# Attention and two MLPs in one launch: the second MLP tile taken from batch 1, plain fp32 P^T V for the early parts, and half-width transposes of the last 64 queries

## The chip, the core and the metric

One core of a Trainium2 chip runs the whole program in one launch. The engines are named as in the profile: PE (TensorE, matmuls and transposes), PEld (its weight loads), DVE (VectorE), ACT (ScalarE), POOL (GpSimd) and SP (SyncE, whose queue issues nearly all transfers). The metric is the device time in microseconds (us).

## The reference

Four batches, eight heads, 576 positions, head size 64; then two MLPs, 512 to 2048 to 512, over all 2304 tokens.

```python
scores = q @ k.T / 8 + minimum(-(cum[i] - cum[j]), 0)   # cum = cumsum(max(s, 0)); causal mask
x = softmax(scores) @ v                                   # -> (2304, 512)
h = x @ w_in;  g = maximum(h, 0) + log1p(exp(-abs(h)));  x = g @ w_out
h = x @ w_in2; P = a0 + a1*h + a2*h*h + a3*h*h*h; Q = 1 + |b0|*|h| + |b1|*h*h
out = (P / (Q + 1e-6)) @ w_out2
```

The MLP weights arrive as 64-bit floats (512 KB for each half of a 128-wide slice of the 2048 hidden features).

## The kernel before

**Numbers on PE.** Most matmuls use the type fp32r. A value that needs more bits is split in two fp32r tiles, a high one (an ACT copy) and a low one (a subtraction on DVE or POOL), and a product is made of three matmuls (the two MLPs) or two (attention, where high and low lie stacked in the 128 rows). A few matmuls take plain fp32 operands ("plain" parts): a matmul of that type appears in the trace as two instructions.

**MLP 1.** A unit is one token tile T and one of 16 feature slices ff: `stage_a` makes h with 12 matmuls, stages 1 to 3 apply the softplus and split it, `stage_b` adds 12 matmuls into the accumulators. The token tiles `T1` have 256, 256 and then four times 448 tokens. The order of the units is T=0 with ff 0 to 7, T=1 with ff 0 to 7, then ff 8 to 15 with T=0 and T=1 in turn, then tiles 2 to 5. Tiles 0 and 1 are the tokens 0 to 255 and 256 to 511 of batch 0. `conv1` turns a 64-bit weight half into a high tile (kept in tag W) and a low tile (written to `l_d` in HBM and fetched again by `stream_l` for later tiles).

**MLP 2** has six tiles of 384 tokens and starts when MLP 1 is nearly done.

**Attention.** A Part is one head and one range of queries. Kind M: queries 0 to 255; L: 0 to 383; B: 256 to 383; H: 384 to 575. `s1` and `s2` make scores and the softmax (DVE minimum and mask, ACT exponential, DVE reciprocal, POOL scaling), `t1` and `t2` transpose the probabilities on PE and `evac_pt` copies them out of PSUM, `pv` multiplies by V. `prep` splits q, k and v in high and low. The parts stand in five segments: M of batch 0 (plain, before any MLP unit); B and H of batch 0; L of batch 1; H of batch 1 with L of batch 2; H of batch 2 with L and H of batch 3. `GROUPS` says over which MLP units a segment is spread: the second over units 0 to 7, the third over units 8 to 31. For kind H, `t2` transposes 128 queries at a time although only the last 64 are new; the copy takes the 64.

**Start.** `load_s0`, `make_cum0` and `load_cum` make the cumulative bias of the first 256 positions of batch 0 and put it as two more rows under q and k of each head, by a transfer from tile to tile. `make_cum` does the same for everything else.

**Order of the work.** `plan` is a list scheduler that simulates all instructions with a table of costs and ties each engine's instructions to the order it found, for those that it starts before a given time (530 us). PSUM has eight banks: four `acc`, two `h`, two `at`. Attention takes `at` and `acc` in turn in the first units (`second_bank`, until unit 10) and `at` alone after.

Of the kernel before, what the change touches and what calls it, by code (L numbers as in the profile page):

```python
# [31 lines left out]
GROUPS = [(0, 8), (8, 24), (32, 16), (48, 16)]  # L32
# [64 lines left out]
class Step:  # L97


    def __init__(self, i, tied):  # L100
# [12 lines left out]
        elif self.engine == "PE":  # L113
            turn = n == 128 and self.ins[0].tile.startswith("ident")
            full = not turn and "32r" not in str(i.ins[0].bass_ap.dtype)
            self.busy = 0.109 if turn else 0.024 + 0.00162 * n if full else 0.012 + 0.000428 * n
# [22 lines left out]
def depend(steps):  # L139
# [4 lines left out]
    for k, s in enumerate(steps):  # L144
# [4 lines left out]
        for x in s.ins + s.outs:  # L149
            if not x.ordered:  # L150
                continue
            write = x in s.outs
            for j, w, y in seen.get(x.tile, ()):
                if (write or w or x.psum and steps[j].engine != s.engine) and x.meets(y):
                    add(j, True)
# [167 lines left out]
def moe_chain_kernel(ctx, tc, qk0, qk, vv, s0, s, w1, w2, ab, out):  # L323
# [62 lines left out]
    class Part:  # L386
        def __init__(self, b, h, kind, rng, first, plain):
            self.b, self.h, self.kind, self.rng = b, h, kind, rng
            self.fresh, self.first, self.plain = rng is not None, first, plain

    def cols(t, rng):
        if rng[0] == "pre":
            return t[:, :, 0:rng[1]]
        return t.rearrange("p a s -> p (a s)")[:, rng[1]:]

# [31 lines left out]
    def load_s0():  # L427
        cum_t["s0"] = sb.tile([2 * H, M + 4], F32, tag="tmp", bufs=1, name="s0_t")
        nc.sync.dma_start(out=cum_t["s0"], in_=s0)

    def make_cum0():
        st, cst = cum_t["s0"][:, 0:M], cum_t["s0"][:, M:M + 4]
        one = t_w("one", [2 * H, M], F32)
        nc.vector.memset(one, 1.0)
        t = t_w("cum0", [2 * H, 2, M], F32)
        nc.vector.tensor_scalar(t[:, 0], st, 0.0, 8.0, op0=ALU.max, op1=ALU.mult)
        nc.vector.tensor_tensor_scan(t[:, 1], one, t[:, 0], 0.0, op0=ALU.mult, op1=ALU.add)
        cum_t["c"] = t_w("cumc", [2 * H, 2, M], F32)
# [3 lines left out]
    def load_s():  # L442
        st = t_w("s_t", [128, S + 6], F32)
        nc.sync.dma_start(out=st, in_=s)
        one = t_w("ones", [128, S], F32)
        nc.gpsimd.memset(one, 1.0)
        cum_t["s"] = (st, one)

    def make_cum():
# [10 lines left out]
        rows = t_q("rows", [128, 2, S], F32R)  # L460
# [5 lines left out]
    def load_pair(i):  # L466
        t = t_w("raw2", [128, 2, 2, M], F32)
        nc.sync.dma_start(out=t[0:64], in_=qk0[i])
        raw2[i] = t

    def load_cum(i):
        for j in range(2):
            h = 2 * i + j
            nc.sync.dma_start(out=raw2[i][64:66, j], in_=cum_t["c"][2 * h:2 * h + 2])

    def load_v0():
        t = t_w("v2", [128, 4, 2, 2, D], F32)
        nc.sync.dma_start(
            out=t.rearrange("p i r c d -> p i (r c d)"),
            in_=vv[0, :, :, 0:2].rearrange("i p r c d -> p i (r c d)"))  # L480
        v2["raw"] = t

    def prep_pair(i):
        for j in range(2):
            op_t[0, 2 * i + j] = (raw2[i][0:66, j], None, v2["raw"][:, i])

    def load_raw(p):
        if p.fresh and p.plain:
# [4 lines left out]
            if p.vkey not in v_t:  # L493
                n = -(-p.rng[1] // 128) if p.rng[0] == "pre" else 5
# [4 lines left out]
        elif p.fresh:  # L499
# [4 lines left out]
            if p.vkey not in v_t:  # L504
                n = -(-p.rng[1] // 128) if p.rng[0] == "pre" else 5
                vr = tmp_tile("R", 2, (128, 5, 2, D))
                nc.sync.dma_start(out=vr[:, 0:n], in_=vv[p.b, p.h // 2, :, 0:n])
                v_t[p.vkey] = [vr, None, n]

    def prep(p):  # L510
        if p.first:
            if p.h % 2 == 0:
                prep_pair(p.h // 2)
        elif p.fresh and not p.plain:
# [3 lines left out]
            if p.rng[0] == "pre":  # L518
                qs = ks = slice(0, p.rng[1])
            else:  # L520
# [56 lines left out]
    def p_tile(p, tag):  # L577
        if p.first:
# [44 lines left out]
    def t1(p):  # L623
        p.pt = (sb.tile([128, 384], F32, tag="pt", bufs=2, name="pt"),) if p.plain else (pt_h[p.idx % 2], pt_l[p.idx % 2])
# [3 lines left out]
        if p.kind in "LM":  # L628
            for i, c0 in enumerate((256, 0, 128)):
                nc.tensor.transpose(bk[:, i * 128:(i + 1) * 128], p.p1[:, c0:c0 + 128], ident)  # L630
            evac_pt(p.pt if p.plain else [t[:, 192:576] for t in p.pt], bk[:, 0:384], nc.scalar)
        else:
            for c in range(4):
                nc.tensor.transpose(bk[:, c * 128:(c + 1) * 128], p.p1[:, c * 128:(c + 1) * 128], ident)
            evac_pt(
                [t[:, 256:1024].rearrange("p (c q) -> p c q", c=4)[:, :, 0:128] for t in p.pt],
                bk.rearrange("p (c q) -> p c q", c=4), nc.scalar)

    def t2(p):
# [3 lines left out]
        if p.kind in "LB":  # L643
            for i in range(3):
                nc.tensor.transpose(bk[:, i * 128:(i + 1) * 128], p.p2[:, i * 128:(i + 1) * 128], ident)
            evac_pt([t[:, 576:960] for t in p.pt], bk[:, 0:384])
        else:

            for i, k0 in reversed(list(enumerate((448, 0, 128, 256, 384)))):
                nc.tensor.transpose(bk[:, i * 64:(i + 2) * 64], p.p2[:, k0:k0 + 128], ident)  # L650
            evac_pt(
                [t[:, 64:1024].rearrange("p (c q) -> p c q", c=5)[:, :, 128:192] for t in p.pt],
                bk[:, 64:384].rearrange("p (c q) -> p c q", c=5))

    def pv(p):
        bk = abank()
        hd = p.h % 2
        ops = []
        for t in p.pt:
            if p.plain:  # L660
                if p.kind == "L":
                    blk = t[:, 64:960].rearrange("p (b q) -> p b q", b=7)
                    ops.append((0, t[:, 320:704], bk[:, 0:384]))
                    ops.append((1, blk[:, 1:6:4, :], bk[:, 128:384].rearrange("p (b q) -> p b q", b=2)))
                    ops.append((2, t[:, 832:960], bk[:, 256:384]))
                elif p.kind == "M":
                    ops.append((0, t[:, 128:384], bk[:, 0:256]))
                    ops.append((1, t[:, 0:128], bk[:, 128:256]))
                elif p.kind == "B":
                    for c in range(3):  # L670
                        ops.append((c, t[:, 576 + c * 128:704 + c * 128], bk[:, 128:256]))
                else:
                    for c in range(4):
                        ops.append((c, t[:, 256 + c * 192:448 + c * 192], bk[:, 64:256]))
                    ops.append((4, t[:, 192:256], bk[:, 192:256]))
# [15 lines left out]
        for i, (c, mv, o) in enumerate(ops):  # L691
            vc = p.vs[:, c] if p.plain else p.vs[:, c, 2 * hd:2 * hd + 2, :]
# [10 lines left out]
        if p.plain:  # L703
# [5 lines left out]

    SPLIT = {  # L710
        "L": [("L", ("pre", 384))],
        "M": [("M", ("pre", 256))],
        "H": [("H", ("suf", 384))],
        "BH": [("B", ("suf", 256)), ("H", None)],
# [3 lines left out]
    def parts_of(lst, first=False, plain=False):  # L718
        return [Part(b, h, k, r, first, plain) for b, heads, kind in lst for h in heads for k, r in SPLIT[kind]]
# [109 lines left out]
    def conv1(ff, half, keep):  # L829
# [5 lines left out]
        if keep:  # L835
            li_t[0, ff, half] = l
            if ff >= NF // 2:
# [46 lines left out]
    def segments(T):  # L884
        t0, m = T1[T]
        o = 0
        while o < m:
            b, s0 = divmod(t0 + o, S)
            n = min(m - o, S - s0)
            yield b, s0, n, o  # L890
            o += n
# [104 lines left out]
    def evacuate(ph, T, acc):  # L996
# [10 lines left out]
        for m, a in enumerate(acc):  # L1007
# [18 lines left out]
            else:  # L1026
                r0 = t0 + m * 128
                nc.sync.dma_start(out=out[r0:r0 + 128, :], in_=yb[:, m % 2])
# [62 lines left out]
    if True:  # L1091
        nc.scalar.preload_act_table_set("natural_log_exp_and_others")
        load_s0()
        load_pair(0)
        load_pair(1)
        load_v0()
        make_cum0()
        load_cum(0)
        load_cum(1)
        for i in (2, 3):  # L1100
            load_pair(i)
# [7 lines left out]
        for i in range(2):  # L1109
            for lst, nm in ((pt_h, "pth"), (pt_l, "ptl")):  # L1110
# [228 lines left out]
```

## Time and profile before

| | |
|---|---|
| median of 3 runs | 1061.16 us (1061.08 to 1062.5) |
| profiled execution | 1063.84 us, span 1062.0 us |
| PE busy | 1022.1 us (96%), 5732 matmuls |
| PEld, DVE, ACT, POOL busy | 923.9, 799.9, 824.1, 462.1 us |
| transfers | 139.43 MB, mean 131 GB/s |
| first unit of tile 0, of tile 2, of MLP 2 on PE | 36.40, 212.28, 663.73 us |

Read the table with care: a PE that counts as busy is not a PE at its peak, because the tail of each matmul, in which the next one already runs, counts too. What a matmul costs is the distance from its start to the next start.

### The profile page before, as it was taken

Reading aid. Unit: us, or ns where it says so; the run is one execution under the profiler, and the core shown is the slowest. Engines: PE = TensorE matmul, PEld = TensorE weight load, DVE = VectorE, ACT = ScalarE, POOL = GpSimd, SP = SyncE. Lnnn points to the kernel's source line nnn. Section 1 sums busy time; section 2 is a strip of 40 time slices with the busy share of each in tenths; the row PEclk is TensorE's granted clock in tenths of the full one; section 3 lists DMA queues with packets and bytes.
Section 4 is the critical chain, followed back from the end, with each engine's and each line's share of the span. In section 5 each row is a group of like instructions: output and inputs, shape, how many; then the busy total and the mean of one; then the engine's idle time right before and its main releaser. Section 6 shows DMA issues by size and latency. Waiting matters only on the chain.

```text
span 1062.0 us, 17769 instructions
## 1 busy us (share of the span) xinstructions
PE 1022.1 (96%) x5732; PEld 923.9 (87%) x5732; DVE 799.9 (75%) x1886; ACT 824.1 (78%) x1748; POOL 462.1 (44%) x509
## 2 busy tenths in 40 slices
PE   5888799999999999999999999999999999999998
PEld 4777699998989888889999888988999999999996
DVE  6898977978886888876666677777676776776765
ACT  5999899987886887875556556787888887888875
POOL 4575365522221122221444575454445454454452
PEclk9899899999999999999999999999999999999999
DMA  6876575755565654415878875110000100000000
GB/s 197 271 240 208 176 239 182 242 168 162 156 179 145 186 172 136 138 56 163 260 232 281 288 248 176 44 31 31 1 31 30 31 31 1 31 31 1 31 1 30
DMA packets 70333, 139.43 MB, mean 131 GB/s; under 512 B 8384, under 2 KB 24144, under 8 KB 70240
## 3 DMA queue, kind: packets, MB, share of 16 engines
q1 hardware_dynamic: 67696, 134.14, 39.3%
q10 hardware_dynamic: 2544, 4.16, 1.6%
q8 instruction: 45, 0.74, 0.3%
q14 instruction: 48, 0.39, 0.1%
HBM read 111.60 MB, written 22.61 MB: 126 GB/s over the span
## 4 chain that ended last, share of the span: by engine, by line
PE 76%; DVE 7%; ACT 6%; DMA 5%; issue 2%; POOL 2%; SPq 0%; POOLq 0%; DVEq 0%; ACTq 0%
PE h L947 7%; PE h L948 7%; PE h L949 7%; PE acc L992 6%; PE acc L990 6%; PE acc L991 6%; PE at L693 5%; PE acc L984 4%; PE acc L985 4%; PE acc L983 4%; PE at L947 4%; PE at L949 4%; PE at L948 3%; DMA raw<-in_w_dram 3%; PE at L569 3%
## 5 line engine op out<-in xcount | busy, mean ns | idle before, releaser
L947 PE MATMUL h<-xs,w1h 128*128 128x448 f32 (+1 forms) x352 | 119.9, 342 | 3.8 <-DVE e L1049 3.8
L949 PE MATMUL h<-xs,w1l 128*128 128x448 f32 (+1 forms) x352 | 118.7, 338 | 1.0 <-POOL w1l L825 1.0
L948 PE MATMUL h<-xs,w1h 128*128 128x448 f32 (+1 forms) x352 | 119.3, 339 | 0.1
L985 PE MATMUL acc<-gh,w1l 128*128 128x448 f32 (+1 forms) x352 | 118.4, 338 | 0.4 <-POOL w1l L825 0.3
L983 PE MATMUL acc<-gh,w1h 128*128 128x448 f32 (+1 forms) x352 | 118.7, 340 | 0.0
L984 PE MATMUL acc<-gl,w1h 128*128 128x448 f32 (+1 forms) x352 | 118.5, 338 | 0.0
L563 POOL TENSOR_SCALAR PA<-PA,stat 128x384 f32<-128x384 f32 (+3 forms) x112 | 71.4, 644 | 102.3 <-DVE stat L562 41.4
L992 PE MATMUL acc<-w2h,gl 128*128 128x512 f32 x288 | 113.5, 394 | 0.0
L990 PE MATMUL acc<-w2h,gh 128*128 128x512 f32 x288 | 113.3, 393 | 0.2 <-ACT gh L1085 0.2
L991 PE MATMUL acc<-w2l,gh 128*128 128x512 f32 x288 | 113.3, 393 | 0.0
L1087 POOL TENSOR_TENSOR gl<-PA,gh 128x384 fp32r<-128x384 f32 x95 | 97.8, 1030 | 6.2 <-ACT gh L1085 5.0
L1058 POOL TENSOR_TENSOR tc<-tc,e 128x384 f32<-128x384 f32 x47 | 51.0, 1085 | 96.4 <-ACT tc L1056 96.4
L563 POOL TENSOR_SCALAR P<-P,stat 128x576 f32<-128x576 f32 x32 | 25.6, 801 | 136.8 <-DVE stat L561 55.6
L947 PEld LDWEIGHTS h<-xs,w1h 128*128 128x128 f32 x352 | 66.6, 190 | 8.5 <-DVE e L1049 5.3
L621 DVE TENSOR_TENSOR ptl<-at,pth 128x320 fp32r<-128x320 f32 (+2 forms) x107 | 60.4, 569 | 15.8 <-ACT pth L620 14.6
L560 ACT ACTIVATE PA<-PA,stat 128x384 f32<-128x384 f32 (+3 forms) x112 | 63.8, 570 | 10.0 <-DVE stat L547 9.5
L949 PEld LDWEIGHTS h<-xs,w1l 128*128 128x128 f32 x352 | 66.4, 188 | 4.2 <-POOL w1l L825 1.3
L984 PEld LDWEIGHTS acc<-gl,w1h 128*128 128x128 f32 x352 | 66.7, 190 | 3.4 <-POOL gl L1087 0.3
L985 PEld LDWEIGHTS acc<-gh,w1l 128*128 128x128 f32 x352 | 66.3, 189 | 3.8 <-POOL w1l L825 0.8
L948 PEld LDWEIGHTS h<-xs,w1h 128*128 128x128 f32 x352 | 66.6, 189 | 3.0 <-DVE xs L917 0.3
L983 PEld LDWEIGHTS acc<-gh,w1h 128*128 128x128 f32 x352 | 66.3, 189 | 2.9
L1085 ACT ACTIVATE gh<-PA 128x384 fp32r<-128x384 f32 x96 | 50.4, 525 | 20.0 <-DVE PA L1073 16.4
(226 smaller groups left out, 3239.6 us busy)
## 6 DMA issues: line engine op xcount, KB each, us to landing
w1l<-l_d SPq DMA_DIRECT2D x148, 256.0 KB
raw<-in_w_dram SPq DMA_DIRECT2D x48, 512.0 KB
raw<-in_qk_dram SPq DMA_DIRECT2D x32, 384.0 KB
l_d<-w1l SPq DMA_DIRECT2D x32, 256.0 KB
raw64x<-in_w_dram SPq DMA_DIRECT2D x16, 512.0 KB
R<-in_vv_dram SPq DMA_DIRECT2D x16, 320.0 KB
raw<-in_qk_dram SPq DMA_DIRECT2D x8, 576.0 KB
out_dram<-yb SPq DMA_DIRECT2D x17, 256.0 KB
```

The costliest lines, as they stand in the source:

```text
L560: nc.scalar.activation(pt[:, 0:n], pt[:, 0:n], AF.Exp, bias=mn, scale=-1.0, accum_out=stat[:, i, 1:2])
L563: nc.gpsimd.tensor_scalar(pt[:, 0:n], pt[:, 0:n], stat[:, i, 2:3], 1.0, op0=ALU.mult, op1=ALU.mult)
L947: nc.tensor.matmul(h, wh[:, cs], xh, start=(k == 0), stop=False)
L948: nc.tensor.matmul(h, wh[:, cs], xl, start=False, stop=False)
L949: nc.tensor.matmul(h, wl[:, cs], xh, start=False, stop=(k == KD - 1))
L983: nc.tensor.matmul(o, wh[:, cs], gh, start=first and not both, stop=False)
L984: nc.tensor.matmul(o, wh[:, cs], gl, start=False, stop=False)
L985: nc.tensor.matmul(o, wl[:, cs], gh, start=False, stop=last and (not both or m % 2 == 1))
L990: nc.tensor.matmul(acc[m], gh[:, cs], wh, start=first, stop=False)
L991: nc.tensor.matmul(acc[m], gh[:, cs], wl, start=False, stop=False)
L992: nc.tensor.matmul(acc[m], gl[:, cs], wh, start=False, stop=last)
L1087: eng.tensor_tensor(gl, g, f(gh), op=ALU.subtract)
```

## The change

Tile 1 of MLP 1 becomes the first 256 tokens of batch 1. The tokens are walked in the order `ORDER`, so tile 2 holds queries 256 to 575 of batch 0 and 256 to 383 of batch 1. Batch 1 gets M parts like those of batch 0 (plain), and its queries 256 to 383 become B parts; its L parts go. The order of units becomes T=0 with ff 0 to 3, T=1 with ff 0 to 3, then ff 4 to 15 with both in turn; M of batch 1 is spread over units 0 to 3, and B and H of batch 0 with B of batch 1 over units 4 to 31. `pv` of M, and of B and H in that segment, works in plain fp32: one copy out of PSUM instead of a split, V used as it is loaded, and the result copied by DVE alone. Two heads of an M pair are added up in one bank (V is loaded with 64 zero columns between the heads), and the bank is split straight into the MLP's input. `t2` of every H part transposes only the rows 64 to 127. At the start the first pair's bias is a matmul of its own (two rows) instead of a transfer; the other pairs' transfers are issued by ACT; the memsets of `ones`, `pth` and `ptl` and `make_cum` come after the first step of the stream. The planner pins the order up to 700 us.

```diff
+ORDER = [(0, 0, 256), (1, 0, 256), (0, 256, 320), (1, 256, 320), (2, 0, S), (3, 0, S)]
+N_S0 = 92
+HF = 4
-GROUPS = [(0, 8), (8, 24), (32, 16), (48, 16)]
+GROUPS = [(0, 4), (4, 28), (32, 16), (48, 16)]
...
+    def fill():
         one = t_w("ones", [128, S], F32)
         nc.gpsimd.memset(one, 1.0)
-        cum_t["s"] = (st, one)
+        cum_t["s"] = (cum_t["s"], one)
+        for i in range(2):
+            for lst, nm in ((pt_h, "pth"), (pt_l, "ptl")):
+                t = t_j(nm, [128, 1024], F32R)
+                nc.gpsimd.memset(f(t[:, 0:192]), 0.0)
+                lst.append(t)
...
     def load_cum(i):
+        eng = nc.scalar if i < 4 else nc.sync
         for j in range(2):
-            h = 2 * i + j
-            nc.sync.dma_start(out=raw2[i][64:66, j], in_=cum_t["c"][2 * h:2 * h + 2])
+            h = 60 + 4 * i + 2 * j
+            eng.dma_start(out=raw2[i][64:66, j], in_=cum_t["c"][h:h + 2])
...
     def scores(o, p, q0, k0, n):
         if p.plain:
-            nc.tensor.matmul(o, p.ht[:, 0, q0:q0 + 128], p.ht[:, 1, k0:k0 + n], start=True, stop=True)
+            nc.tensor.matmul(
+                o, p.ht[:, 0, q0:q0 + 128], p.ht[:, 1, k0:k0 + n], start=True, stop=p.st is None)
+            if p.st is not None:
+                c = cum_t["c"][p.st:p.st + 2]
+                nc.tensor.matmul(o, c[:, 0, q0:q0 + 128], c[:, 1, k0:k0 + n], start=False, stop=True)
             return
...
-            for i, k0 in reversed(list(enumerate((448, 0, 128, 256, 384)))):
-                nc.tensor.transpose(bk[:, i * 64:(i + 2) * 64], p.p2[:, k0:k0 + 128], ident)
+            for i, k0 in enumerate((448, 0, 128, 256, 384)):
+                nc.tensor.transpose(bk[:, (i + 1) * 64:(i + 2) * 64], p.p2[64:128, k0:k0 + 128], ident[64:128, 64:128])
...
+    def pv_first(p):
+        hd, t = p.h % 2, p.pt[0]
+        if hd == 0:
+            pair_bank[p.b] = abank()
+        bk = pair_bank[p.b]
+        for c, mv, o in ((0, t[:, 128:384], bk[:, 0:256]), (1, t[:, 0:128], bk[:, 128:256])):
+            nc.tensor.matmul(
+                o, p.vs[:, c, hd:hd + 2, :].rearrange("p a d -> p (a d)"), mv,
+                start=hd == 0 and c == 0, stop=hd == 1 and c == 1)
+        if hd == 1:
+            t = t_xs([128, 2, 256])
+            nc.scalar.activation(t[:, 0], bk[:, 0:256], AF.Copy)
+            nc.vector.tensor_tensor(t[:, 1], bk[:, 0:256], f(t[:, 0]), op=ALU.subtract)
+            xs_t[0, p.b, p.h // 2] = (t[:, 0], t[:, 1])
...
-        parts_of([(0, R8, "M")], True, True),
-        parts_of([(0, R8, "BH")], False, False),
-        parts_of([(1, R8, "L")], False, False),
+        parts_of([(0, R8, "M")], True, True, True),
+        parts_of([(1, R8, "M")], True, True, True),
+        parts_of([(0, R8, "BH")], False, False, True) + parts_of([(1, R8, "B")], False, False, True),
...
-            at_bank[0] = second_bank if i < 8 + LAGS[0] else at_only
+            at_bank[0] = second_bank if i < HF + LAGS[0] else at_only
...
-    for line in plan(nc.cur_bb.bb.instructions, tied, 530.0):
+    for line in plan(nc.cur_bb.bb.instructions, tied, 700.0):
```

## Rows read from the trace of the kernel before

**Rows 1.** The page's first part: busy time, share of the span, instructions.

```profile
PE 1022.1 (96%) x5732; PEld 923.9 (87%) x5732; DVE 799.9 (75%) x1886; ACT 824.1 (78%) x1748; POOL 462.1 (44%) x509
```

**Rows 2.** Busy time by stretch: length, engines (instructions), clock, DMA share, GB/s.

```profile
0.00:36.40 36.40, 23.39 (x95) 18.16 (x96) 24.21 (x93) 22.15 (x59) 17.20 (x33) 0.95 0.69 224
36.40:132.30 95.90, 79.77 (x535) 71.12 (x533) 87.61 (x259) 86.57 (x207) 56.46 (x54) 0.93 0.67 217
132.30:150.00 17.70, 17.35 (x141) 17.15 (x142) 13.90 (x39) 17.55 (x50) 10.50 (x13) 1.00 0.72 218
150.00:212.28 62.28, 61.12 (x499) 60.32 (x497) 51.92 (x138) 56.98 (x151) 38.48 (x44) 1.00 0.67 220
212.28:480.00 267.72, 267.24 (x1608) 237.09 (x1607) 213.77 (x681) 215.25 (x488) 58.20 (x96) 1.00 0.50 149
```

**Rows 3.** Timeline of PE at 23, 212 and 215 us: start, busy.

```profile
22.94 0.82 PE L567 MATMUL at<-raw 66*128 66x128 f32 x4
...
212.28 0.37 PE L947 MATMUL h<-xs,w1h 128*128 128x448 f32 x1
...
215.15 0.71 PE L650 MATMUL at<-ident,P 128*128 128x128 f32 x5
215.62 0.36 PE L983 MATMUL acc<-gh,w1h 128*128 128x256 f32 x1
215.82 0.28 PE L984 MATMUL acc<-gl,w1h 128*128 128x256 f32 x1
215.94 0.28 PE L985 MATMUL acc<-gh,w1l 128*128 128x256 f32 x1
```

**Rows 4.** Groups of ACT instructions, 0 to 212.28 us: busy, mean ns, idle before.

```profile
L620 ACT ACTIVATE pth<-at 128x384 fp32r<-128x384 f32 x19 | 9.0, 484 | 0.8 <-PE at L645 0.3 <-PE at L630 0.3
L538 ACT ACTIVATE vs<-R 128x640 fp32r<-128x640 f32 x6 | 4.2, 724 | 0.0
L707 ACT ACTIVATE tmp<-at 64x384 f32<-64x384 f32 x8 | 3.9, 486 | 0.2
L620 ACT ACTIVATE pth<-at 128x320 fp32r<-128x320 f32 x5 | 2.1, 428 | 0.8 <-PE at L650 0.8
```

**Rows 5.** Groups of DVE instructions, the same stretch.

```profile
L621 DVE TENSOR_TENSOR ptl<-at,pth 128x384 fp32r<-128x384 f32 x19 | 10.3, 551 | 2.3 <-ACT pth L620 2.3
L539 DVE TENSOR_TENSOR vs<-R,vs 128x640 fp32r<-128x640 f32 x6 | 5.4, 915 | 0.7 <-ACT vs L538 0.5
L708 DVE TENSOR_TENSOR x<-at,tmp 64x384 f32<-64x384 f32 x8 | 4.4, 550 | 2.0 <-ACT tmp L707 2.0
L621 DVE TENSOR_TENSOR ptl<-acc,pth 128x512 fp32r<-128x512 f32 x5 | 3.4, 684 | 0.1
```

**Rows 6.** Timeline of the first 15 us, all engines.

```profile
2.47 0.58 POOL L1112 MEMSET ptl<- 128x576 f32 x1
2.60 2.15 DVE L436 TENSOR_SCALAR cum<-s_t 16x256 f32<-16x256 f32 x1 [1.47 <-DMA s_t<-in_s_dram]
...
5.50 0.40 DVE L440 TENSOR_SCALAR cumc<-cum,s_t 16x256 f32<-16x256 f32 x1
6.13 2.62 SPq L474 DMA_DIRECT2D raw<-cumc  x4
...
8.06 1.62 PE L567 MATMUL acc<-raw 66*128 66x128 f32 x4 [8.06 <-DMA raw<-cumc]
...
12.79 0.97 SPq L799 DMA_DIRECT2D raw<-in_w_dram  x2
```

**Rows 7.** The chain that ended last, 36.4 to 132.3 us: start, us, what.

```profile
37.37 5.03 DMA raw<-in_w_dram
...
113.28 6.17 DMA raw<-in_w_dram
```

**Rows 8.** PE's longest waits, 36.4 to 132.3 us: total us, times, longest.

```profile
PE at L650 <- POOL P L563: 4.4, 3, 2.0
```

**Rows 9.** Transfers, 0 to 212.28 us: total, then issues with count and size.

```profile
DMA packets 19933, 46.51 MB, mean 219 GB/s; under 512 B 2295, under 2 KB 5447, under 8 KB 19910
...
w1l<-l_d SPq DMA_DIRECT2D x26, 256.0 KB
```

More of the change, by code (lines that the diff above doesn't have):

```diff
@@ L113, in __init__ @@
         elif self.engine == "PE":
-            turn = n == 128 and self.ins[0].tile.startswith("ident")
+            turn = self.ins[0].tile.startswith("ident")
             full = not turn and "32r" not in str(i.ins[0].bass_ap.dtype)
-            self.busy = 0.109 if turn else 0.024 + 0.00162 * n if full else 0.012 + 0.000428 * n
+            self.busy = 0.00085 * n if turn else 0.024 + 0.00162 * n if full else 0.012 + 0.000428 * n
             self.done = self.busy + 0.165
@@ L577, in p_tile @@
     def p_tile(p, tag):
-        if p.first:
+        if p.first and p.b == 0:
             return tmp_tile(tag, 3)
@@ L623, in t1 @@
     def t1(p):
-        p.pt = (sb.tile([128, 384], F32, tag="pt", bufs=2, name="pt"),) if p.plain else (pt_h[p.idx % 2], pt_l[p.idx % 2])
+        if p.pv_plain:
+            p.pt = (sb.tile([128, 960], F32, tag="pt", bufs=2, name="pt"),)
+        else:
+            p.pt = (pt_h[p.idx % 2], pt_l[p.idx % 2])
         if p.kind == "B":
@@ L630, in t1 @@
                 nc.tensor.transpose(bk[:, i * 128:(i + 1) * 128], p.p1[:, c0:c0 + 128], ident)
-            evac_pt(p.pt if p.plain else [t[:, 192:576] for t in p.pt], bk[:, 0:384], nc.scalar)
+            evac_pt([t[:, 0:384] if p.first else t[:, 192:576] for t in p.pt], bk[:, 0:384], nc.scalar)
         else:
@@ L659, in pv @@
         for t in p.pt:
[L660 to L675, printed above, removed]
+            if p.pv_plain and p.kind == "B":
+                for c in range(3):
+                    ops.append((c, t[:, c * 128:(c + 1) * 128], bk[:, 128:256]))
+            elif p.pv_plain:
+                for c in range(4):
+                    ops.append((c, t[:, 64 + c * 192:256 + c * 192], bk[:, 64:256]))
+                ops.append((4, t[:, 0:64], bk[:, 192:256]))
             elif p.kind == "L":
@@ L884, in segments, with tokens @@
     def segments(T):
[L885 to L891, printed above, removed]
+        return tokens(*T1[T])
+    def tokens(t0, m):
+        base = 0
+        for b, s0, n in ORDER:
+            lo, hi = max(t0, base), min(t0 + m, base + n)
+            if lo < hi:
+                yield b, s0 + lo - base, hi - lo, lo - t0
+            base += n
     def pieces(t0, m):
@@ L1151, in moe_chain_kernel @@
         gate = {}
-        with ahead(P_CUM):
-            make_cum()
+        load_s()
         for n in range(n_st):
+            if n == 1:
+                last = {i.engine: i for i in traced()}
+                k0 = len(nc.cur_bb.bb.instructions)
+                fill()
+                queue_behind({nc.gpsimd.engine: last[nc.gpsimd.engine]}, k0)
+                with ahead(P_CUM):
+                    make_cum()
             is_prep = stream[n][0] is prep
```

129 lines of the change are left out of this document (72 added, 57 removed).

## The prediction, made before the changed kernel was run

> **What bounds the kernel now.** I read the page first. PE counts as busy for 96% of the span [rows 1], so there is little to win by filling holes unless they lie together. The second view, busy time by stretch, shows that they do. The edges are where PE starts the first unit of tile 0, where the first unit of tile 1 starts, 150, and where tile 2 starts. From 150 us on PE is busy without a break worth naming (61.12 of 62.28 us, then 267.24 of 267.72); before 132 us it is not, and there DVE and ACT are the fuller ones: 87.61 and 86.57 of 95.90 us [rows 2]. In that stretch the B and H parts of batch 0 must end before tile 1 can begin, and each head of them passes many DVE and ACT instructions.
>
> Busy time flatters PE, so I turned to the timeline for the distance between starts. A 256-column fp32r matmul counts 0.28 us but the next starts 0.12 us later (tail 0.16 us, cost 0.47 ns a column). Five transposes and one such matmul lie between 215.15 and 215.82 us: 0.67 - 0.12 = 0.55, or 0.11 us for a transpose of 128. One plain head's scores, 128 and 256 columns, count 0.82 us at 22.94; without the tail 0.66, or 1.72 ns a column [rows 3].
>
> With these the work that PE must do between 36.40 and 212.28 us can be added up. A unit of tiles 0 and 1 is 24 x 0.12 = 2.88 us, 32 of them 92.2. Per head, B is 0.36 (scores) + 0.33 (three transposes) + 0.72 (P^T V, 6 x 0.12) = 1.41; H is 1.02 (512 columns twice, 288 four times, at 0.47 ns) + 0.99 (nine) + 1.20 (ten) = 3.21; L is 0.84 (256 four times, 384 twice) + 0.66 + 0.84 (256 four times, 384 twice) = 2.34; eight of each 55.7. Together 147.9 of 175.9 us: **28 us are lost**, nearly all before 132 us.
>
> **The change part by part.** *PE work of that stretch.* Batch 1 replaces L (2.34) by M, 0.66 + 0.33 + 0.66 = 1.65, and B with plain P^T V of 3 x 128 columns, 0.36 + 0.33 + 0.66 = 1.35: +0.66 a head, +5.3. For batch 0, B's P^T V goes from 0.72 to 0.66; H's from ten matmuls, 1.20, to 4 x 192 and 64 plain columns, 1.43; its five narrow transposes I take at 0.06 instead of 0.11 (see below), -0.25. That is -0.08 a head, -0.6. New total 147.9 + 5.3 - 0.6 = 152.6 us: **the change makes PE's own work in this stretch longer by nearly 5 us**, and can only win by what PE loses there.
>
> *ACT.* Gone for batch 0 are the copies of 384 and 320 columns in `evac_pt` (0.484 and 0.428, x8 each: 7.3), the copies to `tmp` of 128 and 192 columns (bounds nothing and 0.486, that of 384; taken at 0.3: 16 x 0.3 = 4.8) and the V splits (4 x 0.724 = 2.9). For batch 1: one 384 copy a head (3.9), one `tmp` copy a head (8 x 0.486 = 3.9), four shorter V splits (at most 0.724, taken at 0.5: 2.0), a slightly shorter q and k copy (0.4) [rows 4]. Together 25 us. The split of x for tiles 0 and 1 becomes the split of eight pair banks, the same count and size: nothing.
>
> *DVE.* Batch 0 loses the 512 subtraction (8 x 0.684 = 5.5), the V splits (4 x 0.915 = 3.7), and the copies of M into x (8 of 256 columns by 64 rows, bounded by nothing and the 0.550 of 384; 0.42: 3.4); the other subtractions and sums turn into copies of the same length. Batch 1 loses one 384 subtraction a head (8 x 0.551 = 4.4), V splits (4 x 0.9 = 3.6), half of the sum of 384 (8 x 0.27 = 2.2) and some of the q split (1.0) [rows 5]. Together 24 us.
>
> So ACT falls from 161 to 136 us in the stretch and DVE from 153 to 129 (sums of the middle three rows), beside 153 of PE work. Per us of PE that is 0.89 and 0.85; in the stretch from 150 to 212 us it was 56.98 / 61.12 = 0.93 and 0.85, and there PE waited for 1.2 of 62.3 us, 2% [rows 2]. The bound moves from ACT and DVE to PE. The order helps too: tile 1 waits only for M of batch 1, 13 us of PE work spread over four units, no longer for eight B and H.
>
> *The start.* DVE L436 takes 2.15 us on 256 columns while POOL writes 576-column memsets; L440, as wide, takes 0.40 when POOL is idle. The memsets move, so some 1.75 us go. PE's first matmul waits until 8.06 us for a transfer issued at 6.13: for the first pair 1.9 us go too. Against that, the two-row matmuls have all the columns of the scores: two heads at 1.3 us each, the pace of the first four matmuls, +2.6, of which the last of the pair's 2.6 delays only the next head. The weights' transfers, now first issued at 12.79 us [rows 6], move ahead of the large load of s. The prep of batch 0's H, ACT and DVE work before 36.40 us, moves out too, and ACT's six new issues move in. Bounds: no gain, and 3.7 us plus what the lighter ACT gives. I take 3: tile 0 starts at 33.4.
>
> *What is lost after that.* Bounds: nothing, and the 28 us of before. The nearest rows are the 2% of the stretch from 150 us, 3 us on 152.6, and the waits for a 512 KB weight half, of which the chain has one of 5.03 and one of 6.17 us [rows 7]; the waits for POOL's scaling ahead of the transposes are small (4.4 us in three) [rows 8]. I keep one weight wait: 8 us. **Tile 2 then starts at 33.4 + 152.6 + 8 = 194.0 us instead of 212.3: -18.3.**
>
> *After tile 2* only the transposes change: 24 H parts of batches 1 to 3, five transposes each, while PE has no holes [rows 2]. If a transpose costs by its moving columns, as fp32r matmuls do, 64 cost 0.055; if by anything else (128 weight columns, the instruction), up to 0.11. I take 0.06: 24 x 5 x 0.05 = **6.0 us**. The rows exclude neither end; what is nearest is that cost follows columns for every matmul form seen. The output's blocks that straddle two batches become one transfer more, at the end of nothing. The planner's later limit (700 us) reorders a stretch in which PE has small holes; I put it at 0, plus or minus 2.
>
> *Sum.* 18.3 + 6.0 = 24.3 us. The profiled execution took 1063.84 us, 2.7 over the median, so 1039.5 in its terms and **1037 us** against 1061.16.
>
> The Trainium skill (TensorE: Matmul & The Clock Gate, LDWEIGHTS) says that a weight load's time goes with the 128 columns and not with the rows, at 1.2 GHz; as an estimate that is 107 ns for either transpose, and the sum by it would be 8 us worse. The trace has 128-column loads under fp32r matmuls 0.12 us apart [rows 3], which agrees with it and excludes nothing.
>
> **The rivals.** *1. The narrow transposes bring nothing* (0.11 us each, bound by what is not their columns). For it: the trace has no moving operand under 128 columns. Against: the above. Price 32 x 0.25 = 8 us: 1045. *2. They cost.* They use rows 64 to 127 alone, between matmuls that use all 128. If the array empties at each change, the tail of 0.16 us shows twice in a group: 32 x 0.32 = 10 us, 1047. For it and against it there is no row. The Trainium skill (TensorEngine Tiling (Array Packing), Key Properties) does say that a change of the tiling mode drains the engine; no row here shows such a change. *3. The transfers become the bound.* Up to tile 2 they move 46.51 MB at 219 GB/s, of which tile 1's second fetch of low halves is some 2 MB that go, with about as much added for V and q, k of batch 1 [rows 9]. At that same mean, 45 MB end at 206 us, -6 instead of -18: 1049. For it: the waits of the chain; against: DMA was 67 to 72% busy [rows 2]. *4. Nothing lost*: tile 2 at 186, 1029. *5. Slower.* From tile 1's opening at unit 4 its accumulators take the last `acc` banks, so B and H of batch 0, which had `at` and `acc` in turn, run on two `at` banks, and plain P^T V holds one for 1.43 us. A head's B, H and B take 11 banks: some 6 us of PE writing them and 6 of readers, so 6 us on two banks. It decides from 17 us a head on ((194 - 60) / 8), three times that; at 21 us tile 2 starts 32 us later than forecast, and the kernel takes 1069. Against it: L and H of later segments run on two banks beside a full PE [rows 2].
>
> **How the numbers follow.** Forecast (1031 to 1043) 0.50; rival 1 0.15; rival 2 0.08; rival 3 0.11; rival 4 0.10; slower 0.06. The range 1024 to 1051 leaves out the slower case, the worse half of rival 3 and a little beyond rival 4, under 2 in 10. A measurement of this kernel tells about 0.2% (2 us) from no change. Faster by more is 0.91, within 0.04 (rival 5 in small), slower 0.05.
>
> **What would show it.** Tile 2's first L947 with 448 columns at 188 to 200 us; ACT and DVE together some 50 us lighter before it; L645 and L650's counterparts 0.055 us apart (rival 1: 0.11; rival 2: a gap of 0.16 us on both sides); first matmul near 4.5 us; from tile 2 to MLP 2's first `stage_b` 6 us shorter than 451 us. The prediction is wrong if PE still has 20 us of holes between tile 0 and tile 2, and the rows then say for whom it waits: a weight half (rival 3) or a bank's reader (rival 5).

## The result, and the profile after

The changed kernel took **1052.12 us** (median of four runs, 1050.44 to 1055.23) beside 1061.75 us for the kernel before on the same chip: a ratio of **0.9912, 95% interval 0.9885 to 0.9939**. It is faster, by 9.6 us, and not by the 24 us that were forecast (1061.16 to 1037); 1052.1 lies 1 us above the range of 1024 to 1051. Its profiled execution took 1055.23 us, span 1053.4, against 1062.0 of the span before. In spans, which the rest uses, 8.6 us were won and 15.7 are missing.

The page's first part, which answers to [rows 1]:

```profile
PE 1026.0 (97%) x5772; PEld 927.3 (88%) x5772; DVE 792.4 (75%) x1854; ACT 800.0 (76%) x1692; POOL 467.5 (44%) x509
```

The changed kernel by stretch (columns as in [rows 2]). The edges are the first unit of tile 0, 65, the 132.3 and 150 of before, tile 2's first unit, and 480:

```profile
0.00:36.23 36.23, 26.76 (x98) 19.84 (x98) 17.31 (x89) 17.38 (x53) 14.47 (x32) 1.00 0.84 245
36.23:65.00 28.77, 27.57 (x193) 24.76 (x192) 22.38 (x93) 27.52 (x81) 21.57 (x28) 1.00 0.75 256
65.00:132.30 67.30, 63.01 (x489) 60.23 (x488) 59.81 (x154) 60.42 (x141) 48.67 (x45) 1.00 0.74 246
132.30:150.00 17.70, 17.62 (x134) 16.42 (x133) 15.33 (x41) 14.36 (x35) 10.67 (x12) 1.00 0.62 198
150.00:206.05 56.05, 52.17 (x402) 50.14 (x401) 41.80 (x120) 42.30 (x103) 25.18 (x28) 0.97 0.47 144
206.05:480.00 273.95, 272.89 (x1643) 241.40 (x1642) 222.54 (x698) 219.55 (x504) 62.30 (x99) 1.00 0.52 155
```

Put beside [rows 2], this says where the gain is and where it isn't. Tile 0 starts at 36.23 us as before (36.40), not at 33.4. From there to tile 2 it takes 169.8 us instead of 175.9; forecast were 160.6. ACT's work in that stretch fell from 161.1 to 144.6 us (the four middle rows summed), DVE's from 153.4 to 139.3. PE is now the fuller engine there, as forecast, but still not full. The stretches are those of one execution, the slowest of its four; where that matters it is said below.

From tile 2 to the first `stage_b` of MLP 2 it takes 449.2 us (206.05 to 655.26) against 450.6 before (212.28 to 662.92), a gain of 1.4 where 6.0 were forecast; the rest of the kernel is another 1.0 us shorter. So the 15.7 missing us are 2.8 at the start, 9.2 between tile 0 and tile 2, and 3.6 after. (The first `stage_b` is L990 at 662.92 us before; the 663.73 in the table ahead is a later matmul of the same step.)

**The transposes.** PE's timeline at the first H part after tile 2, narrow, in the changed kernel:

```profile
208.49 0.60 PE L667 MATMUL at<-ident,PA 128*128 128x128 f32 x4
209.02 0.52 PE L684 MATMUL at<-ident,P 64*128 64x64 f32 x5
209.47 0.38 PE L1032 MATMUL acc<-gh,w1h 128*128 128x256 f32 x1
209.69 0.28 PE L1033 MATMUL acc<-gl,w1h 128*128 128x256 f32 x1
209.81 0.28 PE L1034 MATMUL acc<-gh,w1l 128*128 128x256 f32 x1
```

Four wide transposes start 0.11 us apart, so the next matmul could start at 208.93; the first narrow one starts at 209.02, **a gap of 0.09 us**. Inside the group they are close, 0.075 us from start to start (0.52 less the 0.22 of the last, over four). The last starts at 209.32 and the next matmul at 209.47, **0.15 us later**; in the wide form [rows 3] the last starts at 215.59 (215.15 and four times 0.11) and the next matmul 0.03 us later, though its successor is then held back by 0.08. Up to the second matmul behind the group it is 0.37 us (209.32 to 209.69) instead of 0.23 (215.59 to 215.82). So 4 x 0.034 = 0.14 us are saved inside and 0.09 + 0.14 = 0.23 paid at the two ends. In the wide form the way from the first of t1's transposes (214.72 us, L634) to the second matmul behind the group (215.82) is 1.10 us; here it is 209.69 - 208.49 = 1.20.

The weight loads of the same place say more about the two gaps:

```profile
208.29 0.56 PEld L667 LDWEIGHTS at<-ident,PA 128*128 128x128 f32 x4
209.02 0.38 PEld L684 LDWEIGHTS at<-ident,P 64*128 64x128 f32 x5 [0.17 <-issue]
209.47 0.19 PEld L1032 LDWEIGHTS acc<-gh,w1h 128*128 128x128 f32 x1
```

L667's loads begin 0.20 us ahead of their matmuls. At both changes, between all rows and rows 64 to 127, the load starts only with its own matmul, at 209.02 and 209.47.

**The start.** Timeline of the first 15 us, which answers to [rows 6]:

```profile
4.29 0.29 DVE L444 TENSOR_SCALAR cum<-s_t 92x256 f32<-92x256 f32 x1 [3.17 <-DMA s_t<-in_s_dram]
...
5.48 0.79 PE L593 MATMUL acc<-raw 64*128 64x128 f32 x2 [5.48 <-DMA raw<-in_qk_dram]
...
5.97 4.25 ACTq L491 DMA_DIRECT2D raw<-cumc  x6
...
6.75 0.38 SPq L498 DMA_DIRECT2D v<-in_v_dram  x1
...
12.37 0.58 SPq L846 DMA_DIRECT2D raw<-in_w_dram  x1
```

And PE's timeline further on:

```profile
15.00 1.65 PE L747 MATMUL acc<-pt,v 128*128 128x256 f32 x4 [0.58 <-ACT pt L645]
...
17.86 1.65 PE L747 MATMUL acc<-pt,v 128*128 128x256 f32 x4 [0.58 <-ACT pt L645]
19.30 1.49 PE L593 MATMUL at<-raw 66*128 66x128 f32 x4
...
31.44 0.82 PE L593 MATMUL acc<-raw 66*128 66x128 f32 x4
32.09 0.84 PE L747 MATMUL acc<-pt,v 128*128 128x256 f32 x4
```

The 2.15 us instruction of [rows 6] now takes 0.29, and PE's first matmul starts 2.6 us sooner, as forecast (5.48; 4.5 was named). But the order puts the third head's scores behind the P^T V of the first two, at 19.30 us; before they ran at 10.75. And a head's scores take 1.28 us from start to start (1.49 less the later tail) until about 30 us, 0.65 from 31 us on: TensorE is at its lower level, 1.2 of 2.4 GHz. The profile holds no clock entry before 30.1 us, where it grants the full level (the clock column shows 1.00 without an entry), so the pace of the matmuls has to be read here. Before, the full level came at 19.1 us, was lost from 25.9 to 29.4, and came back.

The first pair's two-row matmuls show the same loss as the narrow transposes, with all columns in use (128 or 256):

```profile
6.06 0.63 PE L593 MATMUL h<-raw 64*128 64x128 f32 x2
6.62 0.79 PE L597 MATMUL acc<-cumc 2*128 2x128 f32 x2
6.62 0.49 PEld L597 LDWEIGHTS acc<-cumc 2*128 2x128 f32 x2 [0.22 <-issue]
7.34 1.22 PE L593 MATMUL acc<-raw 64*128 64x256 f32 x2
```

Where the rows stay the same, two instructions of 128 columns take 0.43 us at this clock (a head's four, 768 columns in all, take 1.28). Around the changes from 64 rows to two and back they take 0.56 (6.06 to 6.62) and 0.72 (6.62 to 7.34), and again the load starts with its matmul. So a change of rows has its price here too, without fewer columns.

**Waits of PE** between tile 0 and tile 2 (total us, times, longest), and the longest of them on PE's timeline with what DVE did then:

```profile
PE at L684 <- POOL P L589: 3.8, 5, 1.3
PE at L722 <- DVE pt L647: 2.8, 2, 1.9
PE at L679 <- POOL PA L589: 1.4, 4, 0.7
...
165.08 0.94 PE L722 MATMUL at<-pt,vr 128*128 128x128 f32 x6 [1.93 <-DVE pt L647]
```

```profile
163.28 1.16 DVE L860 TENSOR_SCALAR tc<-raw 128x512 int32<-128x512 int32 x1 [2.18 <-DMA raw<-in_w_dram]
164.47 0.56 DVE L647 COPY pt<-at 128x384 f32<-128x384 f32 x1
```

A weight half is late, `conv1` holds DVE, and the copy that PE needs stands behind it. Between 163.2 and 166.6 us PE was busy for 1.52 us, and from 166.6 to 170.0 us it was granted the lower clock (by stretch):

```profile
163.20:166.60 3.40, 1.52 (x13) 1.52 (x14) 3.23 (x8) 1.37 (x5) 0.96 (x1) 1.00 0.38 137
166.60:170.00 3.40, 3.40 (x19) 3.40 (x18) 2.00 (x6) 2.27 (x5) 3.19 (x3) 0.50 0.39 116
```

### The profile page after: what moved, and what is told of

Read it like the earlier page. It is cut to its first block, busy times and chain, and to the rows that moved or that the text cites. A ratio compares the mean times of both kernels' runs of the same rounds, so it can differ in the third digit from the quotient of the medians.

```text
span 1053.4 us, 17780 instructions
## 1 busy us (share of the span) xinstructions
PE 1026.0 (97%) x5772; PEld 927.3 (88%) x5772; DVE 792.4 (75%) x1854; ACT 800.0 (76%) x1692; POOL 467.5 (44%) x509
## 4 chain that ended last, share of the span: by engine, by line
PE 73%; DVE 9%; ACT 9%; POOL 3%; issue 3%; DMA 2%; POOLq 0%; DVEq 0%; ACTq 0%; SPq 0%
PE h L997 7%; PE h L996 7%; PE h L998 7%; PE acc L1041 5%; PE at L722 5%; PE acc L1039 5%; PE acc L1040 5%; PE acc L1033 5%; PE acc L1032 5%; PE acc L1034 4%; PE at L998 3%; PE at L997 3%; PE at L996 3%; PE at L599 3%; PE at L600 2%
## 5 line engine op out<-in xcount | busy, mean ns | idle before, releaser
L1136 POOL TENSOR_TENSOR gl<-PA,gh 128x384 fp32r<-128x384 f32 x95 | 98.0, 1031 | 14.5 <-issue 10.5
L1136 POOL TENSOR_TENSOR gl<-e,gh 128x256 fp32r<-128x256 f32 (+1 forms) x48 | 47.9, 998 | 42.8 <-ACT gh L1134 28.0
```

The source lines that it names most:

```text
L1136: eng.tensor_tensor(gl, g, f(gh), op=ALU.subtract)
```

## The experiments

They were timed in four sets, each beside the kernel before, which had medians of 1062.73, 1064.01, 1064.41 and 1064.06 us there; the ratios are to it, with 95% intervals, and are the safer comparison between sets. "Work" below is PE's, by the distances between starts: 0.46 ns a column for fp32r, 0.108 and 0.075 us for the two transposes, the full-clock price for plain matmuls. By it the stretch from tile 0 to tile 2 held 141.8 us of work and 34 lost before (the prediction had 147.9 and 28), and 149.2 and 20.6 after.

**1. Wide transposes in the changed kernel**. The order on every engine is that of the changed kernel: the planner's table keeps the cost that it had for the narrow ones.

```diff
-            for i, k0 in enumerate((448, 0, 128, 256, 384)):
-                nc.tensor.transpose(bk[:, (i + 1) * 64:(i + 2) * 64], p.p2[64:128, k0:k0 + 128], ident[64:128, 64:128])
+            for i, k0 in reversed(list(enumerate((448, 0, 128, 256, 384)))):
+                nc.tensor.transpose(bk[:, i * 64:(i + 2) * 64], p.p2[:, k0:k0 + 128], ident)
```

> The changed kernel with the last 64 queries transposed 128 wide again, as before the change; the planner is told the narrow cost, so every engine keeps its order to the instruction. Theory now: a group of five narrow transposes costs 0.65 us (0.09 before it, 0.075 from start to start, the rest at its end) against 0.55 us for five wide ones, so this kernel is about 32 x 0.1 = 3 us faster than the changed one (near 1049). Rival, the step of my prediction: a narrow transpose saves half, so this kernel is 6 to 8 us slower than the changed one (near 1059).

Measured: 1048.36 us, ratio 0.9860 [0.9839, 0.9881], which does not touch the interval of the changed kernel. The wide form is 3.8 us faster by the medians. Timeline of PE in this kernel at the same place, and the loads of the group:

```profile
205.14 0.60 PE L667 MATMUL at<-ident,PA 128*128 128x128 f32 x4
205.57 0.71 PE L684 MATMUL at<-ident,P 128*128 128x128 f32 x5
206.03 0.36 PE L1032 MATMUL acc<-gh,w1h 128*128 128x256 f32 x1
206.24 0.28 PE L1033 MATMUL acc<-gl,w1h 128*128 128x256 f32 x1
...
205.46 0.58 PEld L684 LDWEIGHTS at<-ident,P 128*128 128x128 f32 x5
```

1.10 us from the first transpose to the second matmul, as before the change; no gap, and the loads run 0.11 us ahead again. By stretch, from tile 0 to tile 2 and from there to MLP 2:

```profile
35.85:202.70 166.85, 159.19 (x1211) 150.86 (x1209) 137.46 (x405) 144.57 (x356) 106.56 (x111) 1.00 0.64 213
202.70:648.58 445.88, 443.35 (x2503) 404.12 (x2502) 344.74 (x867) 322.21 (x694) 152.53 (x182) 1.00 0.60 191
```

From tile 2 to MLP 2 it takes 445.9 us instead of 449.2. In the other kernels made from the changed one it is 445.3 to 446.2 us with wide transposes (447.4 in experiment 6), and 447.9 and 448.0 in the two with narrow ones (experiments 3 and 4). The step on the transposes falls.

**2. Narrow transposes in the kernel before**: the reverse edit, alone, with the order of before.

> The kernel before with the narrow transposes alone; the planner is told the wide cost, so every engine keeps the order of before. Theory: 32 groups at 0.1 us more, about 3 us slower than before (near 1065), less in the stretch where PE has holes anyway. Rival, my prediction's step: 6 to 8 us faster (near 1055).

Measured: 1067.47 us, ratio 1.0049 [1.0029, 1.0069]: slower, by 5 us. Part of that is the clock: runs with a mean granted clock of 0.990 to 0.992 in both kernels have medians 3.4 us apart. The profiled execution took 1063.89 us, so its stretches show less of it: 452.6 us from tile 2 to MLP 2 instead of 450.6. Both directions agree in sign.

**3. The start of before in the changed kernel**: all pairs' biases by transfers on SP's queue, no two-row matmuls.

```diff
-        for i in range(4):
-            load_pair(i)
+        load_pair(0)
+        load_pair(1)
...
+        load_cum(0)
+        load_cum(1)
+        for i in (2, 3):
+            load_pair(i)
```

> The changed kernel with the loads of the start as before: two pairs of q and k, then V, then the bias rows of every head by SP's queue, and no two-row matmuls; the memsets stay late. Theory: in the changed kernel the third head's scores start at 19.3 us because they stand behind the first heads' P^T V on PE, ordered so because the planner thinks their bias rows land late; here they stand ahead, start before 12 us, the first unit of tile 0 starts near 33 us instead of 36.2, and the kernel is about 3 us faster than the changed one (near 1049). Rival: ACT's and DVE's work until tile 0 sets its start anyway: no earlier than 35.5 us, and the same time as the changed kernel within 1 us.

Measured: 1053.62 us, 0.9904 [0.9880, 0.9928]. The planner sent two weight halves ahead of the bias rows, so PE's first matmul started at 11.59 us; this was not the test that I wanted. It shows something else: PE begins 6 us later than in the changed kernel and tile 0 still starts at 35.74 us (36.23). The first matmul does not set tile 0's start.

**4. The planner's limit back at 530 us**, the changed kernel otherwise.

> The changed kernel with the planner's limit at 530 us as before. My prediction put the limit at 0, plus or minus 2 us. If it is behind the 2 to 3 us that the stretch from tile 2 to the second MLP won in spite of the dearer transposes, this kernel is 2 to 3 us slower than the changed one (near 1055) and PE's holes between 480 and 655 us come back to those of before; if not, it is the same within 1 us.

Measured: 1050.65 us, 0.9886 [0.9865, 0.9908]; 1.5 us under the changed kernel, and the intervals overlap by about half. The limit is worth nothing that can be told, as forecast. Up to tile 2 PE has the same order in both. This profile has no halved clock at 166 us and takes 166.7 us from tile 0 to tile 2 with the narrow transposes, so the 169.8 above hold some 3 us of that one execution (the wait at 163 us and the clock behind it).

From here on the experiments stand on the kernel of experiment 1.

**5. PE kept busy early by plain matmuls**: five fp32 matmuls of 256 columns of ones before the first scores; nothing reads their result.

```diff
+        w = bank("h")
+        for _ in range(5):
+            nc.tensor.matmul(w[:, 0:256], cum_t["one"][:, 0:128], cum_t["one"], start=True, stop=True)
```

> The kernel of e1_full_width with five plain matmuls of 256 columns on a tile of ones ahead of the first scores; their result is not used. In e1_full_width PE's clock is first granted in full at 29.0 us, and until then the M parts cost twice (1.28 us for a head's scores). Theory: that, and not the loads or the first matmul's time, sets when tile 0 starts; with PE at work from 1.3 us on, the full clock comes well before 20 us, tile 0 starts near 30 us instead of 35.9, and the kernel is 4 to 6 us faster than e1_full_width (near 1043). Rival: ACT and DVE (weights, softmax) hold tile 0 back, it starts at 34 us or later and the kernel is within 2 us of e1_full_width.

Measured: 1049.52 us, 0.9863 [0.9847, 0.9878]: nothing. PE was busy for 8.82 of the first 10 us, and the full clock still came at 29.7 us; tile 0 started at 36.36. So the start at full clock was not tested.

**6. The split of P^T V back in for B and H**, which returns ACT's and DVE's copies and splits but leaves the new order of the units. (The memsets of `pth` and `ptl` are 576 columns wide again for it, and tile 0 starts 1.5 us later.)

```diff
-        parts_of([(0, R8, "BH")], False, False, True) + parts_of([(1, R8, "B")], False, False, True),
+        parts_of([(0, R8, "BH")], False, False, False) + parts_of([(1, R8, "B")], False, False, False),
```

> The kernel of e1_full_width with the P^T V of B and H of batch 0 and of B of batch 1 in split fp32r again (high and low copies, V split, the sum of two halves), the rest as there. That gives ACT some 20 us and DVE some 13 us more between tile 0 and tile 2, and PE about the same. Theory of my prediction: ACT and DVE bound that stretch, so tile 2 starts 8 to 15 us later and the kernel is as much slower than e1_full_width (near 1059). Rival: the gain came from the order, tile 1 no longer behind eight B and H; then 0 to 4 us (near 1050).

Measured: 1055.63 us, 0.9925 [0.9908, 0.9942], 7.3 us over experiment 1, of which 5.4 lie between tile 0 and tile 2 (172.2 us instead of 166.8). That is between the two expectations: the relief of ACT and DVE is worth some 5 us there. By stretch, ACT in this kernel has 160.59 us of work there, as much as before (161.1), and PE 148.0 of work instead of 141.8; yet it takes 172.2 us instead of 175.9:

```profile
37.35:209.58 172.23, 159.73 (x1203) 148.88 (x1202) 149.71 (x413) 160.59 (x406) 100.99 (x109) 1.00 0.63 208
```

So the rest of the gain there, 3.7 us in spite of 6 us more work, comes with the order: tile 1 waits for M of batch 1 only. How much of it is the order's own and how much the clock is not shown: before, 13.4 us of this stretch were at the lower clock [rows 2], here none.

**7. Batch 1's B parts between batch 0's**.

```diff
+        [q for h in R8 for q in parts_of([(0, [h], "BH"), (1, [h], "B")], False, False, True)],
```

> The kernel of e1_full_width with the B of batch 1 put behind B and H of batch 0 head by head, instead of after all eight. In e1_full_width ACT and DVE are at 88 to 90% from 65 to 132 us and at 79 and 74% from 150 to 180. Theory: what PE still loses lies where ACT and DVE are full, so spreading B evens it out and tile 2 starts 2 to 5 us earlier (near 1045). Rival: the holes are waits inside one part's own chain (POOL's scaling before the transposes, 5 us in ten waits), which the mix does not change: the same within 1 us.

Measured: 1050.05 us, 0.9867 [0.9854, 0.9881], 1.7 us over experiment 1 by the medians, with intervals that overlap. The place of these parts matters little.

**8. The start of before, with SP's queue tied**: experiment 3 with the first transfers kept ahead of the weights.

```diff
+    queue_behind({nc.sync.engine: order[0][nc.sync.engine]}, order[1])
```

> The kernel of e1_full_width with the loads of the start as before the change (as in e4_start_before) and every later transfer of SP's queue tied behind the last bias transfer, so that no weight is sent ahead of them. The first matmul should come near 7 us and the third head's scores before 11 us, instead of 19.3. Theory that PE's order at the start sets tile 0's start: 33 us or earlier, and 2 to 3 us faster than e1_full_width (near 1046). Rival: at the halved clock the eight M heads take 8 x 3.2 = 25.6 us of PE whatever their order, so tile 0 starts no earlier than 34.5 us and the time is that of e1_full_width within 1.5 us.

Measured: 1047.63 us, 0.9851 [0.9826, 0.9877]. The third head's scores start at 11.40 us instead of 19.3 and tile 0 at 33.42 instead of 35.85, but the next stretch takes 168.4 us instead of 166.8: the total cannot be told from experiment 1. Timeline of PE:

```profile
11.40 1.49 PE L592 MATMUL at<-raw 66*128 66x128 f32 x4
16.76 2.77 PE L592 MATMUL acc<-raw 66*128 66x128 f32 x8
```

The order of the start was worth 2.4 us there, and most of it was given back. The full clock also came sooner, at 25.55 us instead of 28.98, so part of the 2.4 may be the clock's.

**9. fp32r matmuls ahead of the first scores**: twelve of 512 columns, results unused.

> The kernel of e1_full_width with twelve fp32r matmuls of 512 columns on a tile of ones ahead of the first scores (unused result). In e6_early_pe plain matmuls there did not bring the full clock before 29.7 us. If fp32r matmuls do, the M heads cost 1.6 us of PE instead of 3.2, and by the theory that the clock bounds the start tile 0 starts at 28 to 32 us and the kernel is 4 to 6 us faster (near 1044). If tile 0 still starts at 35 us with the full clock granted early, the clock was not the bound. If the clock stays halved until 29 us, the question stays open.

Measured: 1047.03 us, 0.9841 [0.9820, 0.9862]. The full clock came at 5.5 us and went at 8.9, until 29.3, and tile 0 started at 35.43, so the question stayed open. By stretch, the clock is the third column from the end:

```profile
5.00:8.00 3.00, 3.00 (x15) 1.89 (x13) 0.82 (x2) 0.60 (x1) 0.00 (x0) 1.00 1.09 197
8.00:10.00 2.00, 2.00 (x8) 1.02 (x8) 0.64 (x4) 0.00 (x0) 0.00 (x0) 0.72 0.77 286
10.00:15.00 5.00, 2.45 (x7) 1.30 (x6) 1.66 (x13) 2.51 (x9) 2.96 (x9) 0.50 0.64 176
15.00:20.00 5.00, 4.42 (x16) 3.57 (x16) 0.91 (x3) 1.42 (x3) 0.00 (x0) 0.50 0.99 330
25.00:30.00 5.00, 5.00 (x21) 4.39 (x21) 3.81 (x16) 2.56 (x8) 3.02 (x5) 0.57 0.92 257
```

**10. Wide transposes with the limit at 530 us**.

> The kernel of e1_full_width with the planner's limit at 530 us as before: the two undoings together. e5_limit_530 was 1 to 2 us better than the changed kernel, inside its interval; if that is real this one is 1 to 2 us faster than e1_full_width (near 1047), else the same within 1 us.

Measured: 1049.22 us, 0.9863 [0.9842, 0.9884], the same as experiment 1, and as experiment 4 says.

**11. The start filled with fp32r matmuls**: experiment 8 with sixteen such matmuls ahead, and one into the bank of each step of the first eight heads before the step writes it.

```diff
+    def fill_pe(p, bk):
+        if p.first and p.b == 0:
+            nc.tensor.matmul(bk, cum_t["r"][:, 0:128], cum_t["r"], start=True, stop=True)
```

> The kernel of e9_start_tied with fp32r matmuls of 512 columns on a tile of ones (unused results) where PE would wait at the start: sixteen ahead of the first scores and one into each bank of the first eight heads before its real matmuls. e10_early_fp32r brought the full clock at 5.5 us but lost it again at 8.9. Theory that the halved clock is what holds the start: the full clock stays from about 5 us on, the M heads cost 1.6 us of PE, tile 0 starts at 26 to 30 us instead of 33.4, and the kernel is 3 to 6 us faster than e9_start_tied (near 1043). Rival: with the full clock tile 0 still starts at 32 us or later, because the softmax chain and the weights set it.

Measured: **1044.07 us, 0.9815 [0.9800, 0.9830]**, the best of all, 8 us under the changed kernel. The full clock came at 5.4 us and stayed to the end of the kernel. Timeline of PE:

```profile
9.88 0.82 PE L592 MATMUL h<-raw 66*128 66x128 f32 x4
10.54 0.82 PE L592 MATMUL at<-raw 66*128 66x128 f32 x4
11.19 0.82 PE L592 MATMUL acc<-raw 66*128 66x128 f32 x4
...
18.55 0.50 PE L613 MATMUL acc<-onesr 128*128 128x512 f32 x1 [1.31 <-DVE stat L572]
...
23.90 0.92 PE L753 MATMUL acc<-pt,v 128*128 128x256 f32 x4 [0.67 <-ACT pt L649]
...
30.51 0.39 PE L1002 MATMUL h<-xs,w1h 128*128 128x256 f32 x1
```

A head's scores take 0.65 us from the second one on, and tile 0 starts at 30.51 us, 2.9 sooner than in experiment 8, though PE does 8 us more work before it (36 unused matmuls of 0.23 us). The next stretch is as long as there (168.2). So the halved clock did hold the start, and the full one, with the order that came with it, won some 3 us: the planner also moved heads (the fourth one's scores start at 11.19 us instead of 16.76), so clock and order are not wholly parted. From 9 us on PE's named waits before tile 0 are 2.7 us, 2.5 of them for the softmax on DVE and ACT. The intervals of experiments 8 and 11 just touch (0.9826 and 0.9830).

**12. The scaling ahead of the transposes on DVE**: H's second tile of batch 0 and all B parts, to take away the waits for POOL.

```diff
-        nc.gpsimd.tensor_scalar(pt[:, 0:n], pt[:, 0:n], stat[:, i, 2:3], 1.0, op0=ALU.mult, op1=ALU.mult)
+        (eng or nc.gpsimd).tensor_scalar(pt[:, 0:n], pt[:, 0:n], stat[:, i, 2:3], 1.0, op0=ALU.mult, op1=ALU.mult)
```

> The kernel of e1_full_width with the scaling of the second probability tile of H of batch 0 and of all B parts on DVE instead of POOL. The longest waits of PE between tile 0 and tile 2 are for POOL's scaling ahead of the transposes (3.8 and 1.4 us there). Theory that these waits are what is left of the loss: tile 2 starts 2 to 5 us earlier (near 1045). Rival: DVE is itself at 87 to 88% in that stretch, 16 more us of work there delay the evacuations and weights, and the time is the same or 1 to 4 us worse.

Measured: 1047.78 us, 0.9851 [0.9834, 0.9867], and 166.2 us from tile 0 to tile 2 instead of 166.8: the same. PE's longest wait has changed its name from POOL to DVE:

```profile
PE at L679 <- DVE PA L589: 2.7, 4, 1.2
```

## Why the prediction was wrong

**The step that failed: the narrow transposes.** The prediction took 0.06 us for a narrow transpose, 32 x 0.25 = 8 us in all (2.0 before tile 2, 6.0 after). Their pace was nearly that, 0.075; what it left out is what rival 2 named, a price at each change between rows 64 to 127 and all rows. The rows show 0.09 us in front of a group and 0.14 behind it, against 0.14 saved inside, so a group costs 0.1 us more instead of 0.25 less: 32 x 0.1 = +3.2 us. The experiments time it whole: 3.8 us by the medians of the changed kernel with and without, 5.2 us alone (0.49% [0.29%, 0.69%] of 1062.7, so 3.1 to 7.3), and 1.4 us by the medians of the pair with the limit at 530 us (experiments 4 and 10). A term of -8 was between +1.4 and +5.2, +3.8 by experiment 1: with that, 11.8 of the 14.5 us between the forecast gain (24.2) and the measured one (9.6 in medians). Rival 2 was right in kind, with 0.23 us where it had 0.32; its time of 1047 was too low by the other terms. The Trainium skill (TensorEngine Tiling (Array Packing), Key Properties) says that changing the tiling mode drains the engine; the gaps agree with it. I had weighed rival 2 at 0.08 against "cost follows columns for every matmul form seen", but none of those forms used rows 64 to 127 alone, so the rows could not speak for this one.

**The start** (3 us forecast, 0.2 measured, 0.55 in experiment 1). The pieces came as forecast: the memsets' 1.75 us, the earlier first matmul. They were on no path: the clock was at its lower level until 30 us, and the planner put later heads behind the first two's P^T V. The scores of the first two heads, with their changes of rows, took PE from 5.48 us to about 11.8, 3.6 us more than two heads of 66 rows (8.06 to 10.75 before) where 2.6 were forecast. Experiment 3 shows that the first matmul may be 6 us later and tile 0 start no later, 8 that another order (with the full clock 3.4 us sooner) is worth 2.4 us, 11 that the full clock from 5.4 us on, with an order that moved too, is worth another 2.9.

**The loss between tile 0 and tile 2** (8 us forecast). In experiment 1 work there is 150.5 us of 166.8: 16 us lost, and 20.6 in the changed kernel's profiled execution (20 was named as a sign of being wrong), of which the late weight half and the halved clock behind it are some 3. The forecast kept one weight wait and the 2% of the fullest stretch; there were several smaller waits instead, for POOL's scaling (5.2 us in nine) and for copies. Experiment 12 shows that taking away the named releaser does not help: PE then waits for DVE ahead of the transposes (2.7 us at L679). What the rest of the 16 us is made of stays open.

**What held.** The direction; PE's work got longer (forecast 4.7 us, by start distances 7.4); the bound moved from ACT and DVE towards PE, and loss fell from 34 to 16 us without the narrow transposes. Experiment 6 splits this: some 5 us from the lighter ACT and DVE, the rest with the order. Part of before's loss was its clock, which the prediction passed over: 0.93 on average over 95.9 us [rows 2], which is 13.4 us at the lower level and up to 6.7 us of PE's time; in experiment 1 none. The relief was smaller than summed (ACT 16.5 us of 25, DVE 14.1 of 24), partly because 4.8 and 6.9 us more fell away before tile 0. The planner's limit was worth 0. Rival 3 (transfers) and rival 5 (two banks) show in no row as the bound: among PE's longest waits there is none for a transfer or for a bank's reader, and DVE's longest for a weight half is 2.2 us. The 16 us still lost speak against rival 4 (nothing lost).

**A sum that hid errors.** Without the narrow transposes the prediction's terms make 24.3 - 8.0 = 16.3 us, and experiment 1's span is 15.5 us shorter than before's. That it comes so near is partly luck, for it gets there by other parts: 0.55 at the start, 9.0 instead of 13.3 up to tile 2, and 5.9 after tile 2 where nothing was forecast (445.9 instead of 450.6 us, 398.0 instead of 399.1). PE's work after tile 2 is the same 440.3 us in both. This last gain is not the planner's limit (experiment 10); its cause is open.

## What to carry to other kernels

In this kernel half the columns was not half the cost, because the operand also left half of the rows unused: count the changes between the two forms, two for each group, and price them before cutting a group of five. The same 64 columns with all 128 rows, which would make no such change, were not tried. A stretch's gain is not the sum of what falls away at its engines: ask at the start which clock PE has, and which head the order lets through first. To learn what an edit in a bundle is worth, take that edit alone out of the changed kernel with the order of all engines held fixed, as experiment 1 does.

## What the runs showed of the hardware that was not expected

- Transposes of rows 64 to 127 with 64 columns start 0.075 us apart, wide ones 0.109; a group of five between matmuls on all rows pays 0.09 us before and 0.14 behind. At each change the weight load starts only with its matmul (209.02 and 209.47 us) and not ahead of it; the changes between 64 rows and two at the start look the same.
- With plain fp32 matmuls and transposes at the start PE was busy for 8.82 of the first 10 us and 9.65 of those from 20 to 30 us (experiment 5), and the full clock came at 29.7 us. Behind twelve and sixteen fp32r matmuls of 512 columns from 1.45 us on, it came at 5.5 and 5.4 us; in experiment 9, with plain work alone behind them, it went again at 8.9. Why is not settled by these runs.
- Work that nothing reads made the kernel faster: 8 us of it on PE in the first 30 us, with the order that the planner found for it, for 3.5 us of the time (1047.63 to 1044.07).
